# A build-time instruction order with a separate allowance for TensorE's users of late transfers, and a larger pace constant of attention behind the MLP

## The chip, the cores and the metric

The kernel runs on one core of a Trainium2 chip, from one launch. The metric is the device time of a launch in microseconds (us). Four runs of the kernel before took 345.0, 347.38, 347.93 and 348.43 us, with a median of 347.66 us. One further execution was profiled; its instructions span 346.3 us and that run took 348.0 us.

## The reference

Causal attention with 16 extra "beacon" keys and values that every query may see, followed by a two-layer MLP with a squared ReLU, all in float32 outside the kernel:

```python
B, H, S, Nb, D = 8, 8, 576, 16, 64        # q, k, v: [B, H, S, D]; beacon_k, beacon_v: [B, H, Nb, D]
k_all = np.concatenate([beacon_k, k], axis=2)
v_all = np.concatenate([beacon_v, v], axis=2)
scores = 1/np.sqrt(D) * q @ k_all.transpose(0, 1, 3, 2)
scores = np.where(causal, -1e9, scores)   # beacons are always visible
a = np.exp(scores - scores.max(-1, keepdims=True))
attn = (a / (a.sum(-1, keepdims=True) + 1e-9)) @ v_all
x = attn.transpose(0, 2, 1, 3).reshape(B * S, H * D)      # 4608 x 512
h = np.maximum(x @ w_in, 0.0)             # w_in 512 x 2048
out = (h * h) @ w_out                     # w_out 2048 x 512, out 4608 x 512
```

## The kernel before, in words

**Two streams of work.** Attention goes by batch (8) and by pair of heads (4 a batch, so pairs p = 0 to 31). The MLP goes by chunks of 512 tokens (9 chunks, j = 0 to 8). A chunk's first layer (L770) is 16 tiles of 4 matmuls, its second layer (L805) 4 token tiles of 16 matmuls. Chunk j can start once the attention outputs of its tokens stand transposed in `xT`; its last token lies in batch j (batch 7 for chunk 8).

**One pair.** TensorE computes scores of both heads into `strip` (L589, two groups of matmuls), ScalarE takes the exponential into `pt` (L604), VectorE masks (L614, L618), TensorE multiplies by the values (L639, 15 matmuls a head; a column of ones in `vb` gives the row sums), VectorE divides (L657, L659) into `xn`. The normalised rows are transposed into `xT` by TensorE for batches 0 to 2 (L707) and by five DMA transposes on SP's queue for batches 3 to 7 (L690, `add_xt`).

**Loads.** Batch 0's first rows come by SP's and ScalarE's queues in three transfers each for k and q (L487, `add_first_loads`); the rest of batch 0 and batch 1 come as strided rows by POOL's queue (L419, `add_part_loads`) and are transposed by TensorE (L451, L454). From batch 2 on, float32 tiles are loaded by SP into eight staging buffers `stg` (L344, `add_load`), cast to bfloat16 by POOL (L299), and q and k are transposed by one DMA transpose each on SP's queue (L376, `add_trans`); the batch's five v tiles are queued behind those two. Beacon keys of batches 0 and 1 are loaded, cast on VectorE (L391), transposed on TensorE (L399) and copied into `kT` (`add_beacon`).

**Who sets the order.** The order of instructions on every engine is fixed when the program is built. `Order.run` is a list scheduler: it plays the program through with given durations, and each engine takes the ready operation of least priority number. Instructions are then emitted in that order; each engine and each queue runs its list strictly in order, with the true waits by semaphore. The planner's times therefore decide only who stands ahead of whom. A transfer is modelled as one shared DMA resource: `dma_free = max(dma_free, now + DMA_LAT) + dma`, and it is seen 1.6 us after that (L157 to L162). The operation's users are released by one "done" event (L96 to L100).

**The pace.** TensorE prefers attention to the MLP by priority, but a pair of batches 1 to 7 is gated (L559 to L562): it becomes a candidate only when planned MLP progress has reached `27.7 * (LEAD + PACE * (p - 4))` us, with `LEAD, PACE = -0.4, 0.225`. A gated operation is still taken when TensorE has no other candidate (L132 to L133).

Of the kernel before, what the change touches and what calls it, by code (L numbers as in the profile page):

```python
# [16 lines left out]
class Op:  # L17
# [1 line left out]

    __slots__ = ("name", "engs", "dur", "emit", "prio", "need", "users", "left", "ready",  # L20
                 "take", "give", "gate", "held", "slots", "dma", "pe_time", "behind", "followers",
                 "sync", "insts")

    def __init__(self, name, engs, dur, emit, prio=0.0, deps=(), take=None, give=None,
                 gate=None, dma=0.0, pe_time=0.0, behind=(), sync=()):
        self.name = name
        self.engs = engs if isinstance(engs, (tuple, list)) else (engs,)
        self.dur = dur
        self.emit = emit
        self.prio = prio  # L30
        self.sync = list(sync)
        self.need = list(deps) + self.sync
        self.users = []
        self.take = (*take, 1)[:3] if take else None
        self.give = give
        self.gate = gate
        self.held = None
        self.slots = []
        self.dma = dma
        self.pe_time = pe_time  # L40
        self.behind = list(behind)
        self.followers = []


class Order:
# [15 lines left out]
    def add(self, *a, **kw):  # L61
        op = Op(*a, **kw)
        op.need = [d for d in op.need if d is not None]
        self.ops.append(op)
        return op

    def run(self):
        engines = ["PE", "ACT", "DVE", "POOL", "SP", "-"]
        for op in self.ops:
            op.left = len(op.need) + len(op.behind)  # L70
            for d in op.need:
                d.users.append(op)
            for d in op.behind:
                d.followers.append(op)
        avail = {e: [] for e in engines}

        def release(op):
            for e in op.engs:
                avail[e].append(op)

        for op in self.ops:
            if op.left == 0:
                release(op)
        free = {e: 2.3 if e == "DVE" else 0.0 for e in engines}
        dma_free = 0.0
        lanes = {"SP": [], "POOL": [], "ACT": []}
        events = [(0.0, 0, None, None)]
        seq = 0
        started = set()
        issued = []  # L90
        now = 0.0
        while events:
            now = events[0][0]
            while events and events[0][0] <= now + 1e-9:
                _, _, kind, op = heapq.heappop(events)
                if kind == "done":  # L96
                    for u in op.users:
                        u.left -= 1
                        if u.left == 0:
                            release(u)  # L100
                elif kind == "give":
                    from_op, which = op.give if isinstance(op.give, tuple) else (op.give, 0)
                    pool, cls = from_op.take[:2]
                    self.pools[pool].append(from_op.slots[which])
                    if cls in self.inuse:
                        self.inuse[cls] -= 1
            again = True
            while again:
                again = False
                for e in engines:  # L110
                    if free[e] > now + 1e-9:
                        continue
                    best = None
                    fallback = None
                    for op in avail[e]:
                        if any(free[x] <= now + 1e-9 for x in op.engs[:op.engs.index(e)]):
                            continue
                        if op.take:
                            pool, cls, need = op.take
                            if len(self.pools[pool]) < need:  # L120
                                continue
                            if cls in self.limits and self.inuse[cls] + need > self.limits[cls]:
                                continue
                        if op.gate is not None and not op.gate(self):
                            if fallback is None or op.prio < fallback.prio:
                                fallback = op
                            continue
                        if op.dma and len(lanes[e]) >= self.DEPTH[e] and lanes[e][-self.DEPTH[e]] > now + 1e-9:
                            continue
                        if best is None or op.prio < best.prio:  # L130
                            best = op
                    if best is None:  # L132
                        best = fallback  # L133
                    if best is None:
                        continue
                    op = best
                    started.add(id(op))
                    for u in op.followers:
                        u.left -= 1
                        if u.left == 0:  # L140
                            release(u)
                    for ee in op.engs:
                        avail[ee].remove(op)
                    if op.take:
                        pool, cls, need = op.take
                        op.slots = [self.pools[pool].pop(0) for _ in range(need)]
                        op.held = (pool, cls, op.slots[0])
                        if cls in self.inuse:
                            self.inuse[cls] += need
                    dur = op.dur[e] if isinstance(op.dur, dict) else op.dur  # L150
                    end = now + dur
                    free[e] = end
                    self.progress += op.pe_time
                    issued.append((op, e, now))
                    seq += 1
                    heapq.heappush(events, (end, seq, "free", op))
                    if op.dma:  # L157
                        dma_free = max(dma_free, now + self.DMA_LAT[e]) + op.dma
                        seen = max(end, dma_free + 1.6)
                        lanes[e].append(seen)  # L160
                        seq += 1
                        heapq.heappush(events, (seen, seq, "free", op))  # L162
                    else:
                        seen = end + self.LAT[e]
                    seq += 1
                    heapq.heappush(events, (seen, seq, "done", op))
                    if op.give is not None:
                        seq += 1
                        heapq.heappush(events, (seen, seq, "give", op))
                    again = True  # L170
        assert len(issued) == len(self.ops), [o.name for o in self.ops if id(o) not in started][:20]
        for op, e, _ in issued:
            if e != "-":
                op.insts = op.emit(e)
                for d in op.sync:
                    for x in op.insts:
                        self.wait_for(x, d.insts[-1])
        self.issued = issued
        return now
# [3 lines left out]
def kernel(  # L183
# [84 lines left out]
        limits={"av": 2, "tp": 2},  # L268
    )
    order.wait_for = wait_for  # L270
    add = order.add

    nc.vector.memset(warm, 0.0)
# [54 lines left out]
    def add_load(b, x, c, prio, behind=[], sync=[]):  # L328
# [34 lines left out]
        if x != "v":  # L363
            if b < NPE + 2:
                deps += [zero_ops[b]]
            else:
                deps += trans[b - 2, x]
        engs = ("POOL", "DVE") if b == 0 and c <= 1 else ("POOL",)
        cast[b, x, c] = add(f"cast{b}{x}{c}", engs, {"DVE": 0.6, "POOL": 0.65}, emit_cast,
                            prio=prio if b else prio - 220.0, deps=deps, give=ld)  # L370

    def add_trans(b, x, prio):
        srcb, dst = (qb, qT) if x == "q" else (kb, kT)
# [7 lines left out]

        deps = [cast[b, x, c] for c in range(NT)]
        deps += [o for p in range(HP * (b - 2), HP * (b - 1)) for o in qk_ops[p]]
        trans[b, x] = [add(f"tr{b}{x}", "SP", 4.1, emit, prio=prio, deps=deps, dma=4.5)]

    def add_beacon(b, prio):
        prio = prio if b else -299.5
# [3 lines left out]
        bk = add(f"bkc{b}", "DVE", 0.4, lambda e: nc.vector.tensor_copy(bks[b % 2], bkf[b % 2]), prio=prio,  # L391
                 deps=[ld])
        cast[b, "bk"] = bk
        box = {}

        def emit_tp(e):
# [15 lines left out]
    def add_part_loads(b, part, prio, after, free, sync=()):  # L412
        t0, np_, ns = parts_of[b][part]
        step = HP // 2
        for pr in range(0, HP, step):
            h = slice(2 * pr, 2 * (pr + step))
            for n, (x, t) in enumerate((("k", k), ("q", q))):
                def emit(e, t=t, x=x, h=h):
# [1 line left out]
                        out=strided_buf(b, x, part)[:, h],  # L420
                        in_=t[b, h, t0:t0 + np_ * ns, :].rearrange("h (p s) d -> p h s d", s=ns))]
                o = add(f"sld{b}{x}{part}.{pr}", "POOL", 0.75, emit, prio=prio + pr + 0.1 * n, behind=after,
                        sync=() if pr or n else sync, deps=free, dma=1.07 if b == 0 else 1.5)
                after = [o]
                for i in range(step):
                    strided[b, part, pr + i, x] = o
# [50 lines left out]
    def add_first_loads():  # L477
# [4 lines left out]
        for lo, hi in ((0, 1), (1, 2), (2, HP)):  # L482
            for n, (x, t) in enumerate((("k", k), ("q", q))):
# [4 lines left out]
                        out=raw[n][:, h],  # L488
                        in_=t[0, h, t0:t0 + np_ * ns, :].rearrange("h (p s) d -> p h s d", s=ns))]

                o = add(f"fld{x}{lo}", ("SP", "ACT")[n], (0.45, 0.55)[n], emit, prio=-300.0 + lo, dma=0.68 * (hi - lo))
                first.append(o)
                for pr in range(lo, hi):
                    def emit_cast(e, x=x, n=n, pr=pr):
# [54 lines left out]
        return SPLIT if b < NSPLIT else WHOLE  # L549

    mlp_chunk_us = 27.7
    LEAD, PACE = -0.4, 0.225
    norm_ops = {}

    def add_pair(b, pr):
# [127 lines left out]
    def add_xt(b):  # L683
        for t in range(NT):
# [5 lines left out]
                nc.sync.dma_start(out=xT[:, :, at:at + n], in_=xn[b % 2][0:n, t, :], transpose=True)  # L690

            deps = [o for i in range(HP) for o in norm_ops[HP * b + i, 0]] + ring_deps(tok, tok + n)
            o = add(f"xt{b}.{t}", "SP", 1.32, emit, prio=-50.0 + b, deps=deps, dma=0.64 * n / 128)
            xt_ops[b, t] = o
            fed.append((o, tok, tok + n))

# [223 lines left out]
```

The softmax here doesn't subtract the row's maximum and nothing guards it: scores larger than these inputs give would overflow.

## Time and profile before

| what | value |
|---|---|
| median of 4 runs | 347.66 us |
| profiled run, and the span of its instructions | 348.0 us, 346.3 us |
| VectorE, ScalarE, POOL busy | 169.1 us, 194.7 us, 90.7 us |
| matmuls of the first and the second MLP layer (L770, L805), busy | 133.2 us, 131.2 us |
| matmuls of scores and of values (L589, L639), busy | 36.0 us, 40.6 us |
| bytes moved, mean rate | 51.88 MB, 150 GB/s |
| q and k DMA transposes (L376), issue to landing, median | 5.9 us, 5.8 us |
| attention output DMA transposes (L690), issue to landing, median | 2.5 us |

Busy time is the union of an engine's instructions, so the groups overlap slightly. A wait is the idle time just before an instruction, put down to whoever ended it. In the timelines "q" behind an engine's name means its queue, on which a DMA is issued. Some matmul records are missing from the trace (L805 shows 551 of 576), and each missing one looks like a short idle gap with no releaser ("issue").

### The profile page before, as it was taken

The numbers are of one execution on the slowest core, as the hardware profiler recorded it, in microseconds if no ns is written. First come the engines' busy times: TensorE is split into PE (matmuls) and PEld (weight loads), VectorE is DVE, ScalarE is ACT, GpSimd is POOL, SyncE is SP. The second block draws the span as 40 slices with busy tenths as digits, with TensorE's granted clock in tenths as the row PEclk, the third lists the DMA queues.
The fourth block names the chain that finished last, engine by engine and source line by source line (L and its number), as shares of the span: only waits on it lengthen the run. The fifth ranks groups of instructions, "written<-read, shape, count | busy, mean of one in ns | idle before, by whom it ended". The sixth has DMA issues, their size and how long they took to land.

```text
span 346.3 us, 7128 instructions
## 1 busy us (share of the span) xinstructions
PE 327.6 (95%) x2829; PEld 174.4 (50%) x2868; DVE 169.1 (49%) x372; ACT 194.7 (56%) x297; POOL 90.7 (26%) x141
## 2 busy tenths in 40 slices
PE   2898999999999999999989999999999999999995
PEld 1576675444554454444446855444554444444442
DVE  6787984158644975384344556456533302401400
ACT  4795674376647765576546655577536416615611
POOL 9843804316414514151053015312000000000000
PEclk9999999999999999999999999999999999999999
DMA  9999969999999999799699979994015011011002
GB/s 168 212 208 210 206 114 209 213 240 205 178 228 210 207 181 175 186 217 187 138 239 208 196 142 209 219 222 106 2 61 130 1 61 62 0 61 63 0 20 102
DMA packets 145291, 51.88 MB, mean 150 GB/s; under 512 B 132458, under 2 KB 140010, under 8 KB 145258
## 3 DMA queue, kind: packets, MB, share of 16 engines
q1 hardware_dynamic: 135741, 42.45, 60.9%
q0 software_dynamic: 8512, 8.49, 14.7%
q10 hardware_dynamic: 1005, 0.49, 0.6%
q8 instruction: 22, 0.36, 0.4%
q14 instruction: 11, 0.09, 0.1%
HBM read 37.22 MB, written 9.44 MB: 135 GB/s over the span
## 4 chain that ended last, share of the span: by engine, by line
PE 71%; DMA 15%; POOL 5%; SPq 5%; issue 2%; ACT 1%; DVE 0%; POOLq 0%; ACTq 0%
PE ps L805 30%; PE ps L770 29%; DMA stg<-in_v_dram 8%; PE ps L639 6%; PE strip L589 5%; DMA qk_area<-in_k_dram 4%; SPq L344 2%; DMA stg<-in_k_dram 2%; SPq L690 2%; DMA stg<-in_q_dram 1%; POOL stg L344 1%; SPq L376 1%; POOL vb L299 1%; POOL w_in L732 1%; POOL qk_area L419 1%
## 5 line engine op out<-in xcount | busy, mean ns | idle before, releaser
L770 PE MATMUL ps<-xT,w_in 128*128 128x512 bf16 (+3 forms) x690 | 133.2, 340 | 0.8 <-DVE qT L299 0.2
L805 PE MATMUL ps<-w_out,g 128*128 128x512 bf16 x551 | 131.2, 379 | 1.9 <-issue 0.8
L604 ACT ACTIVATE pt<-strip 128x832 bf16<-128x832 f32 (+4 forms) x128 | 103.6, 867 | 40.8 <-PE strip L589 40.7
L786 ACT ACTIVATE g<-ps 128x512 bf16<-128x512 f32 (+2 forms) x128 | 71.9, 562 | 47.3 <-PE ps L770 46.9
L770 PEld LDWEIGHTS <-w_in 128*128 128x128 bf16 x704 | 65.2, 98 | 56.2 <-issue 5.1
L795 DVE TENSOR_TENSOR g<-g 128x1024 bf16<-128x1024 bf16 (+2 forms) x80 | 51.9, 653 | 76.7 <-ACT g L786 75.5
L805 PEld LDWEIGHTS <-g 128*128 128x128 bf16 x576 | 52.5, 98 | 60.7 <-issue 3.8
L299 POOL CAST qk_area<-stg 128x512 bf16<-128x512 f32 (+2 forms) x60 | 40.1, 673 | 54.7 <-DMA stg<-in_k_dram 32.3
L299 POOL CAST vb<-stg 128x512 bf16<-128x512 f32 (+1 forms) x38 | 25.7, 682 | 86.1 <-DMA stg<-in_v_dram 74.8
L639 PEld LDWEIGHTS <-pt 128*128 128x128 bf16 (+1 forms) x960 | 36.5, 98 | 15.6 <-issue 5.4
L297 ACT COPY osb<-ps 128x512 f32<-128x512 f32 x26 | 15.2, 586 | 50.8 <-PE ps L805 44.5
L639 PE MATMUL ps<-vb,pt 128*128 128x65 bf16 (+1 forms) x960 | 40.6, 194 | 2.7 <-POOL vb L299 2.5
L589 PE MATMUL strip<-qT,kT 64*128 64x80 bf16 (+7 forms) x400 | 36.0, 283 | 2.1 <-ACT pt L604 0.9
L659 DVE TENSOR_TENSOR xn<-ps,rcp 128x320 bf16<-128x320 f32 (+2 forms) x64 | 31.5, 492 | 2.5 <-DVE rcp L657 0.2
L614 DVE TENSOR_TENSOR pt<-pt,tri 128x1024 bf16<-128x1024 bf16 (+1 forms) x36 | 24.3, 674 | 13.5 <-ACT pt L604 13.5
L657 DVE RECIPROCAL rcp<-ps 128x5 f32<-128x5 f32 (+2 forms) x64 | 12.3, 191 | 33.5 <-PE ps L639 33.1
L788 DVE TENSOR_SCALAR g<-ps 128x512 bf16<-128x512 f32 (+2 forms) x32 | 19.0, 598 | 10.1 <-PE ps L770 9.6
L589 PEld LDWEIGHTS <-kT 64*128 64x128 bf16 x400 | 12.8, 95 | 21.5 <-issue 17.3
L299 DVE COPY osb<-ps 128x512 f32<-128x512 f32 x10 | 6.9, 692 | 14.9 <-PE ps L805 9.9
L618 DVE TENSOR_TENSOR pt<-pt,tri 80x160 bf16<-80x160 bf16 x32 | 12.4, 389 | 0.0
L344 POOL DMA_DIRECT2D stg<-in_v_dram x10 | 8.5, 852 | 7.1 <-DMA w_in<-in_moe_w_in_dram 5.6
L451 PE MATMUL ps<-ident,qk_area 120*128 120x120 bf16 x16 | 2.3, 300 | 6.2 <-DVE qk_area L299 6.1
(39 smaller groups left out, 68.7 us busy)
## 6 DMA issues: line engine op xcount, KB each, us to landing
out_dram<-osb SPq DMA_DIRECT2D x17, 512.0 KB, 3.8
stg<-in_q_dram SPq DMA_DIRECT2D x24, 256.0 KB, 5.2
stg<-in_k_dram SPq DMA_DIRECT2D x18, 256.0 KB, 5.3
stg<-in_v_dram SPq DMA_DIRECT2D x18, 256.0 KB, 4.5
w_in<-in_moe_w_in_dram POOLq DMA_DIRECT2D x4, 512.0 KB, 11.2
w_out<-in_moe_w_out_dram POOLq DMA_DIRECT2D x4, 512.0 KB, 10.7
stg<-in_v_dram POOLq DMA_DIRECT2D x6, 256.0 KB, 8.5
stg<-in_k_dram SPq DMA_DIRECT2D x6, 224.0 KB, 4.3
```

The source lines that it names most:

```text
L299: eng[e].tensor_copy(dst, src)
L344: insts.append(queue.dma_start(out=st[lo:rows], in_=t[b, :, t0:t0 + rows - lo, :].transpose([1, 0, 2])))
L589: nc.tensor.matmul(st[:, hj, at:at + t1 - t0], kT[b % 2][hp, pr, 128 * c:128 * c + 128], qT[b % 2][hp, pr, t0:t1], start=True, stop=True,)
L604: nc.scalar.activation(pt[take_pt.held[2]][:, :, off:off + width], st[:, :, 0:width], AF.Exp, bias=0.0, scale=scale)
L614: nc.vector.tensor_tensor(out=d, in0=d, in1=tri[:, m0:m0 + m, :][:, None].to_broadcast([128, 2, m, 128]), op=ALU.min)
L639: nc.tensor.matmul(a[:, at + (t - tl[0]) * (D + 1):at + (t - tl[0] + 1) * (D + 1)], P[0:rr, hj, o:o + 128], vb[b % 2][0:rr, c, 2 * pr + hj ...
L659: nc.vector.tensor_tensor(out=xn[b % 2].rearrange("p t (h d) -> p h t d", d=D)[:, h0:h0 + nh, tl[0]:tl[0] + nt], in0=a[:, :, :, 0:D], in1= ...
L770: nc.tensor.matmul(h[:, lo - spans[0][0]:hi - spans[0][0]], w_in_sb[:, mc, ft * 128:(ft + 1) * 128], xT[:, mc, lo % RING:lo % RING + hi - lo],
L786: nc.scalar.activation(dst, h, AF.Relu, bias=0.0, scale=1.0)
L788: nc.vector.tensor_scalar(out=dst, in0=h, scalar1=0.0, scalar2=None, op0=ALU.max)
L795: nc.vector.tensor_tensor(out=d, in0=d, in1=d, op=ALU.mult)
L805: nc.tensor.matmul(o, G[:, fc, ts * 128:(ts + 1) * 128], w_out_sb[:, fc, :], start=(fc == 0), stop=(fc == NFT - 1))
```

## The change

Five things change in the planner's data; no operation is added or taken away, and no size.

1. An operation can carry `late`. Its users on TensorE are released `late` us after its other users. Casts of v for batches 1 to 7 get 2.0, the q and k DMA transposes 3.0, batch 1's strided loads 1.5, the attention output DMA transposes 0.5.
2. The planned DMA cost of a q or k transpose goes from 4.5 to 3.7, of batch 0's second part loads from 1.07 to 0.95.
3. The planned DMA costs of batch 0's first six transfers go from 0.68 (twice) and 1.36 for both k and q to 0.1, 1.7, 0.4 for k and 0.8, 0.5, 1.45 for q.
4. Batch 1's beacon cast also needs, in the plan, the first-phase normalisation of batch 0's last pair.
5. `PACE` goes from 0.225 to 0.255.

```diff
     def __init__(self, name, engs, dur, emit, prio=0.0, deps=(), take=None, give=None,
-                 gate=None, dma=0.0, pe_time=0.0, behind=(), sync=()):
+                 gate=None, dma=0.0, pe_time=0.0, behind=(), sync=(), late=0.0):
...
-                if kind == "done":
+                if kind in ("done", "done_pe"):
                     for u in op.users:
-                        u.left -= 1
-                        if u.left == 0:
-                            release(u)
+                        if ("PE" in u.engs) == (kind == "done_pe"):
+                            u.left -= 1
+                            if u.left == 0:
+                                release(u)
...
                     heapq.heappush(events, (seen, seq, "done", op))
+                    seq += 1
+                    heapq.heappush(events, (seen + op.late, seq, "done_pe", op))
...
         cast[b, x, c] = add(f"cast{b}{x}{c}", engs, {"DVE": 0.6, "POOL": 0.65}, emit_cast,
-                            prio=prio if b else prio - 220.0, deps=deps, give=ld)
+                            prio=prio if b else prio - 220.0, deps=deps, give=ld,
+                            late=2.0 if x == "v" and b > 0 else 0.0)
...
-        trans[b, x] = [add(f"tr{b}{x}", "SP", 4.1, emit, prio=prio, deps=deps, dma=4.5)]
+        trans[b, x] = [add(f"tr{b}{x}", "SP", 4.1, emit, prio=prio, deps=deps, dma=3.7, late=3.0)]
...
         cast[b, "bk"] = bk
+        if b:
+            bk.need.extend(norm_ops[HP - 1, 0])
...
-                        sync=() if pr or n else sync, deps=free, dma=1.07 if b == 0 else 1.5)
+                        sync=() if pr or n else sync, deps=free, dma=0.95 if b == 0 else 1.5, late=1.5 if b else 0.0)
...
-                o = add(f"fld{x}{lo}", ("SP", "ACT")[n], (0.45, 0.55)[n], emit, prio=-300.0 + lo, dma=0.68 * (hi - lo))
+                o = add(f"fld{x}{lo}", ("SP", "ACT")[n], (0.45, 0.55)[n], emit, prio=-300.0 + lo, dma={"k": (0.1, 1.7, 0.4), "q": (0.8, 0.5, 1.45)}[x][min(lo, 2)])
...
-    LEAD, PACE = -0.4, 0.225
+    LEAD, PACE = -0.4, 0.255
...
-            o = add(f"xt{b}.{t}", "SP", 1.32, emit, prio=-50.0 + b, deps=deps, dma=0.64 * n / 128)
+            o = add(f"xt{b}.{t}", "SP", 1.32, emit, prio=-50.0 + b, deps=deps, dma=0.64 * n / 128, late=0.5)
```

More of the change, by code (lines that the diff above doesn't have):

```diff
@@ L21 @@
                  "take", "give", "gate", "held", "slots", "dma", "pe_time", "behind", "followers",
-                 "sync", "insts")
+                 "sync", "insts", "late")
     def __init__(self, name, engs, dur, emit, prio=0.0, deps=(), take=None, give=None,
-                 gate=None, dma=0.0, pe_time=0.0, behind=(), sync=()):
+                 gate=None, dma=0.0, pe_time=0.0, behind=(), sync=(), late=0.0):
         self.name = name
+        self.late = late
         self.engs = engs if isinstance(engs, (tuple, list)) else (engs,)
```

## The prediction

> **What bounds the kernel now.** I read the page's busy times first, then the waits of TensorE, then the windows of 10 us, then the timelines around the waits. The page and the windows (columns: window, its length, then busy time and instruction count of PE, PEld, DVE, ACT, POOL, then granted clock, DMA share, GB/s):
>
> ```profile
> PE 327.6 (95%) x2829; PEld 174.4 (50%) x2868; DVE 169.1 (49%) x372; ACT 194.7 (56%) x297; POOL 90.7 (26%) x141
> PEclk9999999999999999999999999999999999999999
> ...
> 0.00:10.00 10.00, 3.31 (x28) 1.86 (x28) 6.50 (x26) 4.38 (x8) 9.26 (x21) 1.00 0.99 173
> 10.00:20.00 10.00, 8.54 (x128) 5.70 (x128) 7.92 (x27) 9.01 (x15) 8.21 (x12) 1.00 1.16 211
> 20.00:30.00 10.00, 9.05 (x170) 7.56 (x170) 7.05 (x23) 7.39 (x14) 3.23 (x5) 1.00 1.27 205
> 80.00:90.00 10.00, 9.14 (x108) 5.29 (x110) 7.59 (x18) 6.36 (x10) 5.35 (x8) 1.00 1.15 205
> 170.00:180.00 10.00, 8.22 (x83) 4.37 (x83) 4.08 (x10) 4.71 (x6) 4.31 (x7) 1.00 1.29 223
> 260.00:270.00 10.00, 9.95 (x47) 4.51 (x46) 3.46 (x5) 6.81 (x12) 0.00 (x0) 1.00 0.43 111
> ```
>
> TensorE is the bound from 30 us on: it is idle 346.3 - 327.6 = 18.7 us, of which 6.7 lie in the first 10 us, 2.4 in 10 to 30, 0.86 in 80 to 90, 1.78 in 170 to 180, and 3.85 after 330, mostly the end (last result copied and stored). The window 260 to 270 is pure MLP at 47 matmuls in 10 us, 0.213 us each, which is what a mixed window reaches too: in the timeline four L805 matmuls go from 93.59 to 94.45 (0.86) between two blocks of L639 of 0.46, with no loss at the change of kind. So mixing attention and MLP costs nothing by itself, and only waits can be won. TensorE's waits (us in total, times, longest):
>
> ```profile
> PE ps L451 <- DVE qk_area L299: 6.1, 3, 4.2
> PE ps L639 <- POOL vb L299: 2.5, 5, 1.0
> PE ps L454 <- DMA qk_area<-in_k_dram: 0.9, 1, 0.9
> PE strip L589 <- ACT pt L604: 0.9, 4, 0.3
> PE strip L589 <- DVE kT L299: 0.5, 1, 0.5
> PE strip L589 <- ACT qT L297: 0.5, 1, 0.5
> PE ps L454 <- DMA qk_area<-in_q_dram: 0.2, 1, 0.2
> ```
>
> The first line is the start, before any data is there. The second is values cast too late: 0.37 at 41.6 us, 0.34 and 0.25 at 81.5 to 82.0, 1.00 and 0.56 at 175. How the last came about:
>
> ```profile
> 160.85 6.41 SPq L690 DMA_TRANSPOSE xT<-xn  x5
> 167.31 4.06 SPq L344 DMA_DIRECT2D stg<-in_v_dram  x4
> ...
> 175.29 0.62 POOL L299 CAST vb<-stg 80x512 bf16<-80x512 f32 x1 [0.26 <-DMA stg<-in_v_dram]
> ...
> 175.09 0.31 PE L639 MATMUL ps<-vb,pt 128*128 128x65 bf16 x5 [1.00 <-POOL vb L299]
> 175.96 0.19 PE L639 MATMUL ps<-vb,pt 80*128 80x65 bf16 x1 [0.56 <-POOL vb L299]
> ```
>
> Five output transposes (6.4 us on SP) stand ahead of four v loads, the last cast ends at 175.9, and TensorE stands with its list in order behind a value matmul, though MLP matmuls were ready.
>
> **The change part by part.** No instruction is added or removed, so the only terms are waits.
>
> *v casts, late 2.0.* Value matmuls of batches 1 to 7 are placed 2.0 us of plan later, with MLP matmuls put before them. The largest shortfall is 1.00 + 0.56 = 1.56 us, the others 0.37 and 0.59, all under 2.0. Gain 2.5; the low end is 0.9 if the 175 one stays because its loads are ordered anew, the high end 2.5. What fills the time is MLP: at 81 us about 24 us of the 55.4 us (2 x 27.7) of chunks 0 and 1 are left, at 175 chunk 3 is in its second layer. Queued behind the moved matmuls are their normalisation and the next use of a `pt` buffer; four of these exist, and no wait on `pt` buffers shows.
>
> *Batch 1's strided loads, late 1.5.* L454 stands 0.95 us at 29.44 and 0.20 at 34.33, the two L454 lines above. 1.5 exceeds both. Cover: first-layer tiles of chunk 0's first 240 tokens, of which nine of 16 are done by 28.2. Gain 1.1, low end 0 if VectorE's copies of those transposes then delay batch 1's first scores.
>
> *q, k transposes: cost 4.5 to 3.7, late 3.0.* Planned time to landing becomes 0.6 + 3.7 + 1.6 = 5.9, the measured median. TensorE's first scores of a batch move by 3.0 - 2 x 0.8 = 1.4 us. No score matmul waits for a transpose in the waits, so there is nothing to win. Cover at the tightest place, chunk 2's start: batch 2's last copy into `xT` ends at 103.3, and TensorE has chunk 1's second layer until 107.3; so 1.4 us cost nothing, and beyond 4.0 each us costs one. The shorter cost brings v loads forward in the plan, so the planned lateness behind them shrinks; this eats into the 2.0 above, not into the measured 1.56.
>
> *Output transposes, late 0.5.* Nothing waits for them now; a chunk's start moves by 0.5 with other work in hand. Zero.
>
> *PACE.* Pair p is held until 27.7 x (-0.4 + PACE x (p - 4)): for p = 31 that is 157.2 us of MLP before and 179.6 after. So attention ends some 22 us later (257.9 to about 280) and the pure MLP at the end shrinks by as much; TensorE's sum is the same. A pair costs TensorE 0.51 + 0.41 (scores) + 2 x 0.46 (values) = 1.84 us, so a batch took 24.9 + 7.4 = 32.3 us by the pace and takes 28.3 + 7.4 = 35.7 after. The load chain's own period is 152.05 to 185.16, 33.1 us (first transposes of batches 5 and 6). It was as slow as the pace, which is why any hitch reached TensorE; after, loads gain about 2.6 us a batch. This makes the 175 wait vanish a second way. The price is less lead: the gate of the last pair of batch j opens 27.7 x (0.655 - 0.02 j) us of MLP before chunk j needs it, 14.3 us for j = 7 and about 15 for j = 6, where it was 36.7 and 34. Priced under the rivals.
>
> *Beacon cast of batch 1 and batch 0's transfer costs.* The cast (0.40 us on VectorE at 10.49) leaves a stretch after which VectorE idles 1.43 us before 12.33, so nothing is won there; its TensorE transposes (0.27) and copy (0.2) are due only at 33 us. The six first transfers land when they land; only the order of casts and copies around them can change. The trace doesn't show that order. Nearest rows: one wait of L451 of 0.93 us at 6.18 and one of 1.00 at 9.15, both for a cast. I take 0, with -1.0 to +1.0 for the range.
>
> *New waits.* A rearranged list may put some matmul ahead of its data anew; nearest row, 0.37 at 41.6. I add one, 0.4.
>
> Sum: -2.5 - 1.1 + 0.4 = -3.2 us on the profiled span, 343.1. The profiled run took 348.0, 0.3 above the median of 347.66; taken off the median this gives **344.4**.
>
> On the clock, the windows show 1.00 throughout, also from 0 to 10 us with TensorE idle for 6.7. The Trainium skill (TensorE: Matmul & The Clock Gate, "What's actually happening") says that an idle window of about 3.4 us halves the clock and takes about as long to undo. By that rule a single starved chunk start of over 3.4 us would cost a further 1.7 us or so; by the windows it would cost its length alone.
>
> The Trainium skill (Perfetto Trace Analysis, "Identifying the Most-Contended Engine") would not trust a busy share of 95% and would look at FLOPs against the peak; the MLP's 19.3 GFLOP at the page's 78.6 TFLOP/s are an estimated 246 us, which would leave 100 us of headroom to attention and waits. The wait rows leave under 4 to this change.
>
> **The rivals.**
> *Waits move (0.22).* The loads are freed by attention (v casts of batch b need the value matmuls of b - 2), so slower attention holds them back too, and the waits reappear elsewhere. For: 10.9 us of POOL's waits end with TensorE's scores. Against: the v casts before 175 waited 7.88 us for DMA, not for a buffer. Time: 0 to -1.2 of the span, 346.5 to 348.
> *Start gains too (0.10).* The order of the first casts fits the landings better and both L451 waits shrink: -1.0 and -0.5 more, 342.9. For: 1.9 us stand there. Against: DVE is busy 6.5 of the first 10 us, and DMA share is 0.99.
> *A chunk starts dry (0.15), slower.* With the shorter lead, `xT` lands after TensorE has run out of MLP. Place: starts of chunks 4 to 7. From a batch's last scores to the `xT` tiles its chunk needs: 148.65 to 165.89 = 17.2 us (batch 4, third tile), 217.29 to 233.06 = 15.8 (batch 6, second), 248.81 to 261.04 = 12.2 (batch 7, first). In hand after: 14.8 + 3 x 1.84 = 20.3 for batch 6 with two following pairs, 14.3 + 1.84 = 16.1 for batch 7. Margin 3 to 5 us; it decides once the chain exceeds 16 (batch 7) or 20 us. What could do it is SP's order: the two q, k transposes (4.0 + 4.5 us) ahead of the output ones. Price 8.5 - 4 = 4.5 us for each chunk so caught, less the 3.2 won elsewhere: one gives +1.3, 349.0; two give +5.8, 353.5. Against: the planner sees its own queue and would place other pairs there.
>
> **How the numbers follow.** The forecast has 0.53: 344.4, own range 342.5 to 346.3 (start -1.0 or +1.0, 175 wait kept +1.6, no new wait -0.4). A change of about 1%, 3.5 us, is what a measurement can tell: faster means under 344.2, slower over 351.1. Of the forecast's 0.53 somewhat under half lies below 344.2, 0.25, plus 0.10 from the start case and 0.01: 0.36. Slower: most of the dry chunk, 0.12. Same: 0.52. The range 342.2 to 350.0 leaves out the worse dry cases and the best start cases.
>
> **What would show it.** In the profile after: L639's wait for `vb` from 2.5 to under 0.5; L454's first wait gone; last value matmul near 280 us; DMA activity ending later than 240; no idle over 1 us at the first L770 of chunks 4 to 7, and PE busy unchanged near 327. Idle before L770 released by an L690 transpose would mean the dry chunk; new idle before L589 or L639 the moved waits; a change in the first 30 us the start.

## The result and the profile after

The changed kernel took 347.71 us (median of 44 runs), the kernel before 346.77 us (63 runs). The ratio is 1.0024, with a 95% interval of 1.0013 to 1.0034: slightly slower, where 0.9% faster was forecast. The profiled executions span 346.0 us after and 346.3 us before.

In the changed file the line numbers are a few higher: scores L597, values L647, first layer L778, second layer L813, TensorE's transposes L715, loads L349, q and k transposes L382, output transposes L698, casts and copies L304 (VectorE, POOL) and L302 (ScalarE). The page of the kernel after, busy times, then its windows of 10 us (window, length, busy time and count of PE, PEld, DVE, ACT, POOL, clock, DMA share, GB/s):

```profile
PE 327.7 (95%) x2828; PEld 174.6 (50%) x2868; DVE 170.4 (49%) x371; ACT 194.7 (56%) x297; POOL 92.7 (27%) x142
...
20.00:30.00 10.00, 9.85 (x165) 8.28 (x162) 7.98 (x27) 7.55 (x16) 4.23 (x6) 1.00 1.27 205
80.00:90.00 10.00, 9.74 (x112) 5.55 (x114) 6.68 (x15) 5.92 (x9) 5.36 (x9) 1.00 1.16 207
100.00:110.00 10.00, 9.07 (x99) 4.76 (x97) 5.15 (x12) 6.01 (x9) 4.41 (x7) 1.00 1.21 247
170.00:180.00 10.00, 9.84 (x79) 4.74 (x80) 2.95 (x7) 4.49 (x7) 4.63 (x7) 1.00 0.92 169
210.00:220.00 10.00, 8.98 (x75) 4.25 (x74) 4.01 (x8) 4.08 (x6) 3.96 (x6) 1.00 0.78 149
```

TensorE's work is the same to 0.1 us. The holes at 29, 81 and 175 us have closed (9.85, 9.74 and 9.84 busy). Others have opened, above all at 90 to 110, 140 to 150 and 210 to 220: 9.26, 9.07, 9.23 and 8.98 busy, where 9.84, 9.70, 9.88 and 9.78 were busy before. The waits of TensorE after (total us, times, longest) say what they are:

```profile
PE ps L459 <- DVE qk_area L304: 4.5, 2, 4.2
PE strip L597 <- ACT qT L302: 2.0, 3, 0.9
PE ps L778 <- DMA xT<-xn: 1.6, 2, 1.0
PE ps L647 <- POOL vb L304: 1.2, 2, 0.7
PE ps L715 <- DVE xn L667: 1.1, 3, 0.7
PE ps L813 <- issue: 1.0, 6, 0.2
PE strip L597 <- DMA kT<-qk_area: 0.6, 1, 0.6
```

Values wait 1.2 us instead of 2.5 and the strided rows no longer show. New are 1.6 us for `xT` (0.66 at 144.0, 0.97 at 217.8: the starts of chunks 3 and 5), 0.58 for a DMA transpose of k at 99.0, and at batch 3's values 0.68 at 107.7. The start has only changed names: scores wait for a copy where the first transposes waited for a cast.

### The profile page after: what moved, and what is told of

Its sections match the earlier page's. It is cut to its first block, busy times and chain, and to the rows that moved or that the text cites. A ratio compares the mean times of both kernels' runs of the same rounds, so it can differ in the third digit from the quotient of the medians.

```text
span 346.0 us, 7107 instructions
## 1 busy us (share of the span) xinstructions
PE 327.7 (95%) x2828; PEld 174.6 (50%) x2868; DVE 170.4 (49%) x371; ACT 194.7 (56%) x297; POOL 92.7 (27%) x142
## 4 chain that ended last, share of the span: by engine, by line
PE 73%; DMA 16%; POOL 5%; SPq 3%; issue 2%; ACT 1%; DVE 0%; POOLq 0%; ACTq 0%
PE ps L778 31%; PE ps L813 30%; DMA stg<-in_v_dram 8%; PE ps L647 6%; PE strip L597 5%; DMA qk_area<-in_k_dram 3%; DMA xT<-xn 2%; DMA stg<-in_q_dram 2%; POOL vb L304 1%; DMA stg<-in_k_dram 1%; SPq L382 1%; POOL stg L349 1%; SPq L349 1%; POOL qk_area L427 1%; POOL qk_area L304 1%
## 5 line engine op out<-in xcount | busy, mean ns | idle before, releaser
L778 PE MATMUL ps<-xT,w_in 128*128 128x512 bf16 (+3 forms) x689 | 133.6, 340 | 2.8 <-DMA xT<-xn 1.6
L813 PE MATMUL ps<-w_out,g 128*128 128x512 bf16 x551 | 130.4, 379 | 1.9 <-issue 1.0
L778 PEld LDWEIGHTS <-w_in 128*128 128x128 bf16 x704 | 64.9, 98 | 58.8 <-issue 8.3
L794 ACT ACTIVATE g<-ps 128x512 bf16<-128x512 f32 (+2 forms) x122 | 68.1, 558 | 43.7 <-PE ps L778 43.0
L813 PEld LDWEIGHTS <-g 128*128 128x128 bf16 x576 | 52.5, 98 | 62.2 <-issue 4.8
L304 POOL CAST qk_area<-stg 128x512 bf16<-128x512 f32 (+2 forms) x60 | 40.3, 679 | 80.3 <-DMA stg<-in_k_dram 63.7
L302 ACT COPY osb<-ps 128x512 f32<-128x512 f32 x31 | 18.2, 586 | 71.4 <-PE ps L813 51.4
L647 PEld LDWEIGHTS <-pt 128*128 128x128 bf16 (+1 forms) x960 | 37.3, 98 | 13.2 <-issue 2.6
L304 POOL CAST vb<-stg 128x512 bf16<-128x512 f32 (+1 forms) x39 | 27.3, 709 | 61.4 <-DMA stg<-in_v_dram 50.7
L647 PE MATMUL ps<-vb,pt 128*128 128x65 bf16 (+1 forms) x960 | 40.5, 194 | 1.4 <-POOL vb L304 1.2
L597 PE MATMUL strip<-qT,kT 64*128 64x80 bf16 (+7 forms) x400 | 36.1, 286 | 2.6 <-ACT qT L302 2.0
L796 DVE TENSOR_SCALAR g<-ps 128x512 bf16<-128x512 f32 (+2 forms) x38 | 23.6, 621 | 17.7 <-PE ps L778 16.4
L597 PEld LDWEIGHTS <-kT 64*128 64x128 bf16 x400 | 12.6, 95 | 20.2 <-issue 14.0
L349 POOL DMA_DIRECT2D stg<-in_v_dram x10 | 8.5, 854 | 6.8 <-DMA w_in<-in_moe_w_in_dram 5.4
L304 DVE COPY kT<-ps 128x576 bf16<-128x576 bf16 (+3 forms) x12 | 6.0, 508 | 2.1 <-PE ps L462 1.1
L715 PE MATMUL ps<-ident,xn 128*128 128x128 bf16 (+2 forms) x60 | 5.8, 215 | 1.2 <-DVE xn L667 1.1
```

Source lines behind the costliest of these rows:

```text
L302: nc.scalar.copy(dst, src)
L304: eng[e].tensor_copy(dst, src)
L597: nc.tensor.matmul(st[:, hj, at:at + t1 - t0], kT[b % 2][hp, pr, 128 * c:128 * c + 128], qT[b % 2][hp, pr, t0:t1], start=True, stop=True,)
L647: nc.tensor.matmul(a[:, at + (t - tl[0]) * (D + 1):at + (t - tl[0] + 1) * (D + 1)], P[0:rr, hj, o:o + 128], vb[b % 2][0:rr, c, 2 * pr + hj ...
L778: nc.tensor.matmul(h[:, lo - spans[0][0]:hi - spans[0][0]], w_in_sb[:, mc, ft * 128:(ft + 1) * 128], xT[:, mc, lo % RING:lo % RING + hi - lo],
L794: nc.scalar.activation(dst, h, AF.Relu, bias=0.0, scale=1.0)
```

## The experiments

Two theories stood first. **A:** the allowances' gain is real and the larger PACE takes it back at chunk starts. **B:** the profiled execution of before had more waiting than most, so there was less to win. Two more, **D** and **E**, came out of the first four runs. All ratios are to the kernel before, run on the same chip, with the 95% interval in brackets; edits are on the kernel before or after, as named. In the diffs the minus lines are that kernel's and the plus lines the run's. Waits are of the one profiled execution of a run.

**e1, the kernel before again** (no edit).

> The kernel before, unchanged, for a second profile. Theory A (the waits that the change removes are in every execution, and the chunk starts take them back): L639's wait for vb is again about 2.5 us and L454's first about 0.9, span 346 +- 0.5. Theory B (the profiled execution of before had more waiting than most; its run took 348.0 against a median of 346.77 over 63 runs): L639's wait for vb is under 1.5 us, the 1.56 us at 175 us is smaller or gone, span about 345.

Ratio 0.9995 [0.9967, 1.0023], span 344.2 us, 2.1 us less than the first profile of the same kernel. Its waits of TensorE for values and strided rows:

```profile
PE ps L639 <- POOL vb L299: 1.4, 4, 0.4
PE ps L454 <- DMA qk_area<-in_k_dram: 0.6, 1, 0.6
```

The 1.56 us at 175 us are not there. B holds as far as it goes: of the 3.6 us that the prediction counted as winnable, 2.0 stood in this execution. It took 345.95 us, less than the median of 346.77, and the first took 348.0, more than it; so a typical execution may hold something between the two.

**e2, PACE alone**, on before.

```diff
-    LEAD, PACE = -0.4, 0.225
+    LEAD, PACE = -0.4, 0.255
```

> The kernel before with PACE 0.255 alone. Theory A (the larger PACE makes xT late at chunk starts, 1.6 us in the profile after): first-layer waits for xT of 1 to 3 us appear and L639's vb waits after 110 us vanish; ratio to before 1.001 to 1.005. Theory B (vb waits are mostly of one execution, so PACE only adds): 1.003 to 1.008. If neither PACE nor xT matters: 0.999 to 1.001.

Ratio 0.9984 [0.9966, 1.0002]. No wait for `xT`; the waits for `vb` are 0.37 at 41, 0.60 at 81 and 0.57 at 109 us, none later. So the larger PACE by itself does not make chunks start dry, and A falls. That it gives later batches a lead fits the missing waits after 110 us, but the second profile of before had only 0.28 us there.

**e3, PACE back to 0.225**, on after (the reverse of that line).

> The changed kernel with PACE back at 0.225. Theory A: without the xT waits the allowances' gain is left, 2 to 3 us, ratio to before 0.991 to 0.995. Theory B: the allowances gain little, 0 to 1 us, ratio 0.997 to 1.000, and no xT wait over 0.3 us shows. If PACE is not the cause of the loss: 1.002 to 1.003 as for the changed kernel.

Ratio 1.0092 [1.0061, 1.0122], worse than the changed kernel, against all three expectations. Waits for `vb` 4.5 us in 6, for `kT` 1.1 in 2; the profiled execution was the slowest of six (351.02, median 349.45). The waits for `xT` are gone, as A had it, and the time is worse all the same. The loss sits in what is left of the change, and PACE was hiding part of it.

**e4, the old start**, on after: first transfers 0.68, second part 1.07, no extra need of the beacon cast.

```diff
-        if b:
-            bk.need.extend(norm_ops[HP - 1, 0])
...
-                        sync=() if pr or n else sync, deps=free, dma=0.95 if b == 0 else 1.5, late=1.5 if b else 0.0)
+                        sync=() if pr or n else sync, deps=free, dma=1.07 if b == 0 else 1.5, late=1.5 if b else 0.0)
...
-                o = add(f"fld{x}{lo}", ("SP", "ACT")[n], (0.45, 0.55)[n], emit, prio=-300.0 + lo, dma={"k": (0.1, 1.7, 0.4), "q": (0.8, 0.5, 1.45)}[x][min(lo, 2)])
+                o = add(f"fld{x}{lo}", ("SP", "ACT")[n], (0.45, 0.55)[n], emit, prio=-300.0 + lo, dma=0.68 * (hi - lo))
```

> The changed kernel with the old planned costs of batch 0's transfers (0.68 and 1.07) and without the beacon's extra need; allowances and PACE as after. Theory A and B both hold the start for nearly neutral: the profile after shows 7.8 us of TensorE idle in the first 30 us against 9.1 before, 0.95 of which the allowance of batch 1's strided loads explains, so ratio to the changed kernel 1.000 to 1.001, to before 1.002 to 1.004. Theory C (the new order of the start costs time that a profile's idle does not show): 0.998 to 1.000 to before.

Ratio 1.0026 [1.0004, 1.0048], the changed kernel's own: the start is neutral in time. But the waits stand elsewhere: TensorE now waits 2.5 us for `vb`, 2.0 of it at 108.4, and not at all for `kT` or `xT`. A small change at the start reorders what follows. So either the allowances lose, or the shorter planned cost of the q and k transposes (3.7 for 4.5) does. That is theory **D** against **E** (the allowances).

**e5, the transpose cost alone put back**, on after.

```diff
-        trans[b, x] = [add(f"tr{b}{x}", "SP", 4.1, emit, prio=prio, deps=deps, dma=3.7, late=3.0)]
+        trans[b, x] = [add(f"tr{b}{x}", "SP", 4.1, emit, prio=prio, deps=deps, dma=4.5, late=3.0)]
```

> The changed kernel with one number put back: the planned DMA cost of a q or k transpose is 4.5 again instead of 3.7. Theory D (the shorter planned cost is what loses: it lets the plan expect the loads of every later batch 1.6 us sooner than the batch before, more than the allowance of 2.0 covers from batch 3 on): L647's waits for vb fall under 0.6 us, the 0.68 at batch 3 is gone; ratio to before 0.993 to 0.997. Theory E (the allowances themselves lose, by moving TensorE's work of a batch later): no better than the changed kernel, 1.001 to 1.004.

Ratio 0.9909 [0.9882, 0.9935], 343.62 us. D holds and E falls: one planned number is worth 1.0024 - 0.9909 = 1.15%, 4 us. The waits of TensorE after the first 30 us, gaps without a releaser left out, are down to one:

```profile
PE ps L647 <- POOL vb L304: 0.6, 1, 0.6
```

What the number did is seen at batch 3. The timelines of TensorE (start, us, what, count, idle before) of after and of e5:

```profile
106.14 0.89 PE L647 MATMUL ps<-vb,pt 128*128 128x65 bf16 x14
107.71 0.19 PE L647 MATMUL ps<-vb,pt 80*128 80x65 bf16 x1 [0.68 <-POOL vb L304]
```

```profile
105.49 2.76 PE L778 MATMUL ps<-xT,w_in 128*128 128x512 bf16 x12
108.19 0.58 PE L597 MATMUL strip<-qT,kT 64*128 64x496 bf16 x4
108.70 1.04 PE L778 MATMUL ps<-xT,w_in 128*128 128x512 bf16 x4
109.57 0.62 PE L647 MATMUL ps<-vb,pt 128*128 128x65 bf16 x15
```

The data come at nearly the same time in both: the k transpose of batch 3 lands at 98.9 after and 98.7 in e5, the last v cast ends at 107.65 and 106.51. But with 3.7 the first scores start at 98.99 (after a stop of 0.58) and the values at 106.14, with 4.5 at 101.61 and 109.57, with MLP matmuls in between: 2.6 and 3.4 us apart, where the data are 0.2 and 1.1 apart.

**e6, the shorter transpose cost alone**, on before.

```diff
-        trans[b, x] = [add(f"tr{b}{x}", "SP", 4.1, emit, prio=prio, deps=deps, dma=4.5)]
+        trans[b, x] = [add(f"tr{b}{x}", "SP", 4.1, emit, prio=prio, deps=deps, dma=3.7)]
```

> The kernel before with the shorter planned transpose cost alone, 3.7 for 4.5. Theory D: value matmuls of batches 3 to 7 stand ahead of their casts; waits for vb 4 us or more in total (1.4 in the second profile of before), ratio 1.006 to 1.015. Theory E: no more than 0.3% from before, waits for vb as before, 1.4 to 2.5 us.

Ratio 1.0110 [1.0081, 1.0140]: D's size, from the other side. The place that was expected, the values, was wrong. TensorE's waits:

```profile
PE strip L589 <- DMA kT<-qk_area: 4.3, 3, 2.3
PE ps L454 <- DMA qk_area<-in_k_dram: 1.3, 1, 1.3
PE ps L639 <- POOL vb L299: 1.0, 4, 0.4
```

With no allowance on the transposes it is the scores that come too early (0.76, 2.29 and 1.28 us, batches 2, 3 and 6), and the values behind them wait no more than 0.4 us at a time. (This was the slowest of the six executions, 351.8 us at a median of 350.35.)

**e7, allowances and PACE without any new transfer cost**, on before (diff of the change without its lines for 3.7, 0.95, the first transfers and the beacon).

> The kernel before with the four allowances and PACE 0.255, all planned DMA costs and the start as before. Theory D: the allowances do what they are for, waits for vb and for strided rows under 0.6 us together; ratio 0.993 to 0.998, below PACE alone (0.9984). Theory E: above PACE alone, 1.000 to 1.004, with waits at scores or at xT in place of those for vb.

Ratio 0.9902 [0.9875, 0.9930], 343.43 us, with 0.61 us at 41.3 the only wait for data after the start over 0.3 us. This is the forecast's size, and the start's costs, present in e5 and absent here, again make no difference. Against e4, from which e7 differs by the planned transpose cost alone (4.5 for 3.7), it is the number's worth a third time: 1.0026 - 0.9902 = 1.24%.

**e8, the same without the allowances on transposes** (3.0 and 0.5 left out).

> As the run with allowances and PACE, but only those of v casts (2.0) and of batch 1's strided rows (1.5); none for transposes. Theory D: the same within 0.2%, since no profile but those with the shorter transpose cost shows TensorE waiting for a q or k transpose. If the allowance of 3.0 for transposes is a cost of its own: faster than that run by 0.2% or more; if it is needed: scores wait for kT or qT by 0.5 us or more.

Ratio 0.9930 [0.9904, 0.9956]. Scores wait for `kT` at 71.8 and 99.1 us, 0.42 and 0.59: these two waits are what the allowance on q and k transposes takes away with 4.5. The expectation that it was idle was wrong by the waits; the two ratios' intervals overlap.

**e9, the allowances alone**, PACE 0.225, on before.

> The kernel before with the four allowances alone: planned transfer costs, start and PACE (0.225) as before. If PACE earns its part only where the plan is too hopeful: ratio to before 0.990 to 0.993, as with PACE 0.255 and the allowances (0.9902). If PACE 0.255 gives the loads a lead that the allowances can't (PACE alone gave 0.9984): 0.993 to 0.997, with waits for vb of 1 us or more after 110 us.

Ratio 0.9942 [0.9916, 0.9969], with 1.2 us of waits for `vb`, 1.0 of it after 200 us. The larger PACE takes these away (e7); its share, about 0.4%, is not clear of the intervals.

**e10, larger allowances on top of 3.7**, on after.

```diff
-                            late=2.0 if x == "v" and b > 0 else 0.0)
+                            late=4.0 if x == "v" and b > 0 else 0.0)
...
-        trans[b, x] = [add(f"tr{b}{x}", "SP", 4.1, emit, prio=prio, deps=deps, dma=3.7, late=3.0)]
+        trans[b, x] = [add(f"tr{b}{x}", "SP", 4.1, emit, prio=prio, deps=deps, dma=3.7, late=5.0)]
```

> The changed kernel, planned transpose cost still 3.7, with larger allowances: v casts 4.0 for 2.0, q and k transposes 5.0 for 3.0. If the shorter cost loses only through TensorE's order (matmuls put ahead of their data): waits for vb and kT vanish but the loads' order on SP stays, ratio 0.990 to 0.994. If it loses through SP's order too (q and k loads put ahead of the output transposes, so that xT is late): the waits for xT of 0.66 and 0.97 us stay, ratio 0.995 to 1.000.

Ratio 1.0007 [0.9988, 1.0026]; waits for `vb` 0.3 us, for `kT` none, but:

```profile
PE ps L778 <- DMA xT<-xn: 1.7, 1, 1.7
PE ps L778 <- DVE osb L304: 1.6, 1, 1.6
```

One is the start of chunk 3, at 142.67; the other the start of chunk 5, at 217.10. The profile names VectorE's copy there, but that was done at 216.25, and the second output tile of batch 5, the last that chunk 5 needs, landed at 217.01: both wait for `xT`. Together they are 3.3 us, as much as the span is longer than that of e5 (345.3 and 342.0). So allowances for TensorE's users alone do not repair the plan. What stands in the way is SP's list, here of the kernel after and of e5, with the first matmuls of chunk 3 (start, us, what, count, idle before):

```profile
130.59 4.54 SPq L349 DMA_DIRECT2D stg<-in_q_dram  x4
135.22 1.09 SPq L349 DMA_DIRECT2D stg<-in_k_dram  x1
136.41 1.11 SPq L349 DMA_DIRECT2D stg<-in_q_dram  x1
137.61 7.12 SPq L698 DMA_TRANSPOSE xT<-xn  x5
144.00 1.02 PE L778 MATMUL ps<-xT,w_in 128*128 128x512 bf16 x4 [0.66 <-DMA xT<-xn]
```

```profile
130.10 1.79 SPq L349 DMA_DIRECT2D stg<-in_q_dram  x2
131.98 7.54 SPq L698 DMA_TRANSPOSE xT<-xn  x5
139.62 0.53 SPq L841 DMA_DIRECT2D out_dram<-osb  x1
140.25 1.54 SPq L349 DMA_DIRECT2D stg<-in_q_dram  x2
141.15 1.03 PE L778 MATMUL ps<-xT,w_in 128*128 128x512 bf16 x4
```

Batch 3's last value matmul ends at 132.89 after, and VectorE has the last normalised rows at 133.66. But with 3.7 seven loads of batch 5 stand ahead of the output transposes on SP from 130.11 on; these go out 3.95 us later, at 137.61, and the third tile lands at 143.86, as chunk 3 wants it (first L778 at 144.0, 0.66 late). With 4.5 four of these seven stand behind, the transposes go out 1.20 us after the rows stand (130.78 and 131.98), the tile lands at 137.35 and chunk 3 starts at 141.15 with no wait. In e10 the same seven loads stand ahead, and it takes 5.60 us (131.32 and 136.92). No run moved the output transposes alone, so this cause rests on the traces.

**e11, a planned transpose cost of 5.3**, on after.

> The changed kernel with a planned transpose cost of 5.3, as far above 4.5 as 3.7 is below. Theory D in its one-sided form (an overestimate only puts ready MLP work first, an underestimate stops TensorE): no wait for vb or kT over 0.6 us, ratio within 0.3% of the run with 4.5 (0.9909), up to 0.994. If the error counts either way: 1.000 or more.

Ratio 0.9939 [0.9916, 0.9961], no wait for `vb`, `kT` or `xT`. An overestimate of 0.8 costs 0.3% against 4.5, within the intervals, and keeps most of the gain; the underestimate of 0.8 costs 1.15%.

**e12, e7 with batch 1's v casts allowed 3.0.**

> The allowances and PACE 0.255 on the kernel before, with batch 1's v casts allowed 3.0 instead of 2.0. The wait of 0.61 us for vb at 41.3 us should go; ratio 0.988 to 0.990, 0.0 to 0.2% below the same without it (0.9902).

Ratio 0.9917 [0.9894, 0.9941]. The wait at 41.3 is gone; 0.58 us for a copy of q at 39.6 stands in its place. Not told apart from e7. The two best versions, e7 and e5, beat both kernels by about 1%.

## Why the prediction was wrong

The step that failed is the one on q and k transposes: "The shorter cost brings v loads forward in the plan, so the planned lateness behind them shrinks; this eats into the 2.0 above, not into the measured 1.56." It was priced at nothing because no score matmul waited for a transpose, the allowances seemed to cover the rest, and the planned 5.9 us to landing then equalled the measured median. That compared one transfer's landing, while the planner uses the number as the time that the shared DMA is taken, so that in the plan every load behind two transposes a batch moves forward. The runs show it worth 1.15% (e5 against the changed kernel), 1.1% (e6 against before) and 1.24% (e7 against e4), each pair differing by this number alone. The profiles show the loss in three places: values ahead of their casts, scores ahead of `kT`, and q and k loads ahead of the output transposes on SP. Which of them takes it differs from run to run: all three after, values in e4 (with a fall of the clock, told below), scores in e6, `xT` in e10. The step took the first two for covered and did not look at the third.

Point by point:

- *What bounds it, and that mixing is free:* right. TensorE's busy time is 327.6 before and 327.7 after, though attention ends at 280.1 us instead of 257.9 (about 280 was said).
- *v casts, 2.5 won:* the sign is right, the size that of one execution. The second profile of before has 1.4 us there, and after it is 1.2; with 4.5 put back it is 0.6, so 0.7 of the 1.2 comes with the shorter transpose cost.
- *Batch 1's strided rows, 1.1 won:* the wait is gone, from 0.9 and 0.2 us, or 0.6 in the second profile.
- *Output transposes, zero:* nothing waited for them before; after, 1.6 us did. By the traces the cause is SP's order, which this step did not look at.
- *PACE:* no wait for `vb` after 110 us in after or e2, where e9 with the old PACE has 1.2; that fits the lead that was forecast.
- *The start, zero:* right (e4 against the changed kernel 1.0026 and 1.0024, e5 against e7 0.9909 and 0.9902).
- *New waits, 0.4:* they are 1.6 + 0.6 + 0.7 = 2.9 us of the 4 us that e5 wins back. This is the term that makes the sum wrong; the rest of the 4 us is not accounted for.
- *The rival of the dry chunk* looked at the right place, `xT` behind SP's order, with a wrong price: 0.66 and 0.97 us for 4.5 each, at chunks 3 (not among those named) and 5, from q and k loads on SP and not from the two q and k transposes. These waits came only where the shorter lead and the shorter transpose cost met (after, e10), and not always then (e4): e2 and e5, with the shorter lead and 4.5, show none, and e3, with 3.7 and the old lead, shows none.
- *The other rivals:* the start gained nothing (e4). Moved waits did come, but not as that rival had it, from slower attention holding loads back: with the same PACE and 4.5 they are gone but for one of 0.6 us (e5, e7).
- *The base:* the first four runs gave 347.66, 63 runs give 346.77, and the profiled run of 348.0 lay above both. The count of what could be won came from a poor execution. (347.66 less 3.2 is 344.46, not 344.4; nothing hangs on it.)

With everything but the one planned number, the parts give the size that the sum said: 346.7 x (1 - 0.9909) = 3.2 us. That is in part luck, since the sum took its waits from a poor execution. From the second profile of before to that of e7 the span falls by 2.7 us (344.2 to 341.5), the waits for `vb` and the strided rows by only 1.4 (2.0 to 0.6).

Open: why 4.5 fits better than 3.7 as the planned cost, when from issue of the q transpose to landing of the k transpose batch 3 takes 9.1 us after and 9.9 in e5. By the planner's formula two transposes that meet no other transfer take 10.0 us with 3.7 (SP 4.1 for the first, then 0.6 + 3.7 + 1.6) and 11.2 with 4.5 (0.6 + 4.5 + 4.5 + 1.6), so the shorter number is not too short for the pair itself. The larger one may stand in for loads planned too short; no run changed those.

## What to carry to other kernels

When a build-time order is fitted to measured transfers, a number that agrees with one measured landing can still make the order worse, and what counts is who stands ahead of whom on every in-order list, the DMA queue's too. Here a cost 0.8 above the best one tried put ready work first and cost 0.3%; one 0.8 below stopped TensorE, the bound engine, and cost over 1%. Take a second profile before adding up waits for transfers: 1.6 of the 3.6 us counted were not in the second.

## What was not expected of the hardware

In the profile of e4 the wait for `vb` at 108.4 us was 1.99 us, followed by one of 0.30, and from 110.0 on TensorE's granted clock was at half for 3.4 us (windows of e4):

```profile
110.00:113.40 3.40, 3.40 (x29) 1.55 (x28) 1.98 (x4) 0.83 (x2) 1.22 (x2) 0.51 1.08 225
113.40:120.00 6.60, 6.60 (x64) 3.27 (x63) 5.35 (x11) 4.92 (x8) 3.76 (x6) 1.00 1.05 232
```

Half the clock over 3.4 us is 1.7 us of matmul time, on top of 2.3 us of waiting. In e6 a wait of 2.29 us at 100.4 left the clock at full. By its length one such fall takes 0.005 off a run's mean granted clock (half of 3.4 us in 346), and the runs' means say that it is no single case: they are 0.993 or 0.994 in four of e4's 12 runs and 0.988 to 0.995 in three of e10's 12, but 0.995 in one of the changed kernel's 44 and never under 0.998 in e6's six. What decides it is not shown. The Trainium skill (TensorE: Matmul & The Clock Gate, "What's actually happening") puts the fall after an idle window of about 3.4 us; here it followed waits of 2.0 and 0.3 us with 0.3 us of matmuls between. The duration of the fall agrees.

The prediction read a clock of 1.00 from the start on, in the windows. Those rows have no clock event under them there: the first event of the kernel before is at 14.9 us, and matmuls tell another story. In its timeline eight L451 of 120 columns stand in 0.98 us from 9.15 on; less the last one's 0.30, that is 0.097 us from one to the next. At the 0.213 us for 512 columns of the window 260 to 270, 120 columns would take 0.050, about half of that. So TensorE ran at half clock there, and probably up to that first event. The same section of that page says that a cold start is at half clock, which agrees.
